# A second layer by block products behind a first layer: sums of x by a written plan, first block products right behind the first layer's last product, y matmuls 8, 10, 8, 10 between groups

## The chip, the cores and the metric

The program runs on one core of a Trainium2 chip. The metric is the time of one execution on the device in microseconds, as the median of runs; lower is better.

## The reference

Windowed attention with sink tokens gives x (1536 tokens, 512 wide). Two feed-forward layers follow, each 512 to 2048 to 512, the first with softplus, the second with hard swish:

```python
def _moe_ref(x, w_in, w_out):
    h = x @ w_in
    g = np.maximum(h, 0.0) + np.log1p(np.exp(-np.abs(h)))
    return (g @ w_out).astype(np.float32)

def _moe2_ref(x, w_in, w_out):
    h = x @ w_in
    relu6 = np.clip(h + 3.0, 0.0, 6.0)
    g = h * relu6 / 6.0
    return (g @ w_out).astype(np.float32)
```

The weights arrive as 64-bit floats.

## The kernel before

Every matmul operand is held as a high and a low half (hi + lo), and each product is made of three passes, hi hi, hi lo and lo hi. `xT` holds x transposed, four blocks of 128 features by 1536 tokens, both halves.

**First layer.** It goes over three token blocks of 512 (0 to 2) and in each over 16 chunks c of 128 hidden features: 48 steps, numbered 0 to 47; step 32 + c is chunk c of the last token block. `stage_a` of a step makes h (12 matmuls, `products`, L148) and the activation (`activate`, L170 to L180): ScalarE runs Abs, Exp, two copies and Ln, POOL makes u (L174), VectorE makes h (L177) and e (L178), ScalarE the high half of g (L179) and POOL the low half (L180). `stage_b` adds g times the second weight into four y banks (12 matmuls, L209), two steps later. Between Ln and L177 a call `filler` puts other work into the queues: in token blocks 1 and 2 that is `Blocks.early`. The four y banks of a token block are split into `xT` at its end (`evac`, L217 ScalarE, L218 VectorE); the second layer reads them there.

**Preparing the second layer.** `early` does three things. `some(n)` converts about n columns of the second layer's weights from 64-bit words on VectorE (L355, L359, L363; 32 weight pieces, and 48 groups of these three instructions, of 512 or 256 columns); L363 writes one tile f, which is written to DRAM (`kept`). `load` reads such pieces back. And in token block 2 the first block product's operands are made: `sums` (POOL, L401) and `left` (ScalarE L389 and POOL L390) from the weights, and `right(0)` from `xT`: eighteen VectorE sums (L451) in slots V and U, and eight splits of them (L389, L390). A split of V is read by ScalarE and POOL before the next sum may overwrite V. `right` is a generator; before, `early` takes two steps of it per chunk from chunk 3 on.

**Second layer.** It works on two halves of 768 tokens (s) with eight pairs of weight chunks each: 16 units (q = 0 to 15). A unit makes the 2 by 2 block product of the pair by seven products M1 to M7 in place of eight (L619, six matmuls of 128 by 384 each), in groups M1 M6, M2 M7, M5 M4, M3. Two PSUM banks take the products in turn, so M2 waits until M1's bank has been read, and so on. VectorE adds the products to the four quadrants of h (L601), and `act` turns a quadrant into g: ScalarE L529, VectorE L532 (its last reader of the bank), ScalarE L534, VectorE L536. Between the groups PE makes the 36 y matmuls of the unit before (`products` of `Blocks`, L571), so many that 11, 21, 31 and 36 of them are done behind the four groups. During units 1 to 7 `right(1)` makes the sums for the second token half, one generator step behind each group and two behind the second. In unit 8 the first half's six y banks are copied out (L589, L591).

At the seam, `Ffn.run(32, 48)` ends with the h of step 47 and the y of step 45; `Blocks.run` takes the 12 y matmuls of step 46 and then starts unit 0, between whose groups the 12 of step 47 stand.

From `with in_order` on, every engine's queue holds its instructions in the order in which the code issues them; the first layer's steps 4 to 31 are put in order by a scheduler.

## Time and profile before

| | us |
|---|---|
| median of 3 runs | 633.97 (632.43 to 636.32) |
| the profiled execution | 633.76 |
| its span, first to last instruction | 631.8 |
| PE busy | 602.9 (95%) |
| VectorE (DVE) busy | 432.4 (68%) |
| ScalarE (ACT) busy | 383.6 (61%) |
| POOL busy | 351.0 (56%) |
| mean granted PE clock | 0.993 |

PE's matmuls are pipelined: a row's duration counts from the first start to the last end, so what a block costs is read from one start to the next. The share of PE is an average; the stages differ, and the rows below are taken by stage. In a timeline row the bracket says how long the engine stood idle before it and what ended that.

### The profile page before, as it was taken

What the parts mean: (1) busy time and instruction counts of PE and PEld (TensorE: products, weight loads), DVE (VectorE), ACT (ScalarE), POOL (GpSimd) and SP (SyncE); (2) the same over time, 40 slices, a digit from 0 to 9 for tenths busy, and PEclk for the clock granted to TensorE, in tenths of its full rate; (3) what the DMA queues carried; (4) which work ended last, traced back from release to release, by engine and by line L of the source; (5) the groups of instructions that cost most, each with busy time, mean ns of one, the idle gap of its engine ahead of it and who ended that gap; (6) DMA issues with size and microseconds to landing.
All of it is one profiled execution on the core that took longest, in us unless ns stands there. A gap on an engine that the chain in (4) does not pass through costs nothing.

```text
span 631.8 us, 10989 instructions
## 1 busy us (share of the span) xinstructions
PE 602.9 (95%) x3863; PEld 509.3 (81%) x3863; DVE 432.4 (68%) x920; ACT 383.6 (61%) x843; POOL 351.0 (56%) x317
## 2 busy tenths in 40 slices
PE   8999999999999999989998869999999989999995
PEld 4888887887888888878876758988799878999984
DVE  6899999998788763377766457776755555555552
ACT  4999977887775566656666544554354444444432
POOL 1021248988544444535586755867786646666631
PEclk9999999999999999999999979999999999999999
DMA  7979869102656660043443210121212241211002
GB/s 218 274 235 279 268 222 365 41 0 93 203 188 198 202 200 1 1 133 101 129 156 115 84 35 33 66 68 67 67 66 67 84 150 67 68 67 34 1 1 106
DMA packets 54592, 75.12 MB, mean 119 GB/s; under 512 B 3904, under 2 KB 32576, under 8 KB 54528
## 3 DMA queue, kind: packets, MB, share of 16 engines
q1 hardware_dynamic: 53840, 74.07, 36.5%
q8 instruction: 32, 0.52, 0.3%
...
## 4 chain that ended last, share of the span: by engine, by line
PE 62%; DVE 13%; ACT 9%; POOL 6%; issue 4%; DMA 4%; SPq 0%; ACTq 0%; DVEq 0%; POOLq 0%
PE bank L619 15%; PE h_w L148 14%; PE y L571 14%; PE y_w L209 13%; PE bank L571 3%; POOL u_w L174 2%; ACT P L935 2%; DMA raw_w<-in_moe_w_in_dram 2%; DVE xs L931 1%; DVE e_w L178 1%; DVE slot_V L451 1%; PE o L973 1%; DVE e L532 1%; ACT e_w L171 1%; ACT u_w L173 1%
## 5 line engine op out<-in xcount | busy, mean ns | idle before, releaser
L209 PE MATMUL y_w<-g_w,w_w 128*128 128x512 f32 x576 | 142.9, 392 | 7.2 <-POOL g_w L180 4.8
L148 PE MATMUL h_w<-xT,w_w 128*128 128x512 f32 x576 | 140.9, 391 | 0.0
L209 PEld LDWEIGHTS y_w<-g_w,w_w 128*128 128x128 f32 x576 | 107.3, 188 | 32.8 <-POOL g_w L180 7.3
L148 PEld LDWEIGHTS h_w<-xT,w_w 128*128 128x128 f32 x576 | 107.6, 188 | 23.4 <-DVE e_w L178 0.9
L529 ACT ACTIVATE e<-bank 128x384 f32<-128x384 f32 x64 | 31.3, 492 | 108.6 <-DVE bank L601 107.7
L180 POOL TENSOR_TENSOR g_w<-e_w,g_w 128x512 fp32r<-128x512 f32 x48 | 62.8, 1308 | 51.2 <-ACT g_w L179 51.0
L174 POOL TENSOR_TENSOR u_w<-u_w,e_w 128x512 f32<-128x512 f32 x48 | 63.5, 1324 | 46.2 <-ACT u_w L173 45.1
L111 POOL TENSOR_TENSOR w_w<-t_w,w_w 128x512 fp32r<-128x512 f32 x32 | 41.4, 1294 | 64.5 <-ACT w_w L110 46.0
L571 PE MATMUL y<-slot_W,slot_G 128*128 128x512 f32 x279 | 72.8, 395 | 0.0
L179 ACT ACTIVATE g_w<-e_w 128x512 fp32r<-128x512 f32 x48 | 30.2, 630 | 62.7 <-DVE e_w L178 55.5
L571 PEld LDWEIGHTS y<-slot_W,slot_G 128*128 128x128 f32 x279 | 52.6, 190 | 10.1
L390 POOL TENSOR_TENSOR slot_B<-slot_S,slot_B 128x512 fp32r<-128x512 f32 x16 | 21.6, 1351 | 59.1 <-ACT slot_B L389 59.1
L177 DVE SCALAR_TENSOR_TENSOR h_w<-h_w,r_w 128x512 f32<-128x512 f32 x48 | 33.4, 695 | 29.3 <-ACT r_w L175 29.3
L571 PE MATMUL y<-slot_W,g 128*128 128x512 f32 x201 | 52.8, 392 | 0.0
L935 ACT ACTIVATE P<-xs,mx 128x208 f32<-128x208 f32 (+1 forms) x96 | 42.6, 447 | 10.6 <-DVE mx L931 10.4
L390 POOL TENSOR_TENSOR slot_W<-slot_O,slot_W 128x512 fp32r<-128x512 f32 x32 | 42.2, 1318 | 11.9 <-ACT slot_W L389 9.6
L571 PEld LDWEIGHTS y<-slot_W,g 128*128 128x128 f32 x201 | 37.5, 188 | 7.2
L532 DVE SCALAR_TENSOR_TENSOR e<-e,bank 128x384 f32<-128x384 f32 x64 | 34.9, 551 | 12.0 <-ACT e L529 11.2
L619 PE MATMUL bank<-xT,slot_C 128*128 128x384 f32 x192 | 39.2, 339 | 3.2 <-DVE e L532 3.2
L178 DVE TENSOR_TENSOR e_w<-h_w,u_w 128x512 f32<-128x512 f32 x48 | 33.1, 689 | 12.6 <-POOL u_w L174 12.0
L619 PE MATMUL bank<-xT,slot_A 128*128 128x384 f32 x192 | 39.3, 339 | 0.0
L619 PEld LDWEIGHTS bank<-xT,slot_C 128*128 128x128 f32 x192 | 34.0, 188 | 5.9 <-DVE e L532 4.9
(133 smaller groups left out, 1172.1 us busy)
## 6 DMA issues: line engine op xcount, KB each, us to landing
...
```

The lines of the kernel that those rows point to most:

```text
L111: nc.gpsimd.tensor_tensor(out=wt[:, 1, :], in0=t.bitcast(F32), in1=wt[:, 0, :].bitcast(F32), op=ALU.subtract)
L148: nc.tensor.matmul(h, wt[:, ws, kk * P : (kk + 1) * P], xT[:, xs, kk, t0 : t0 + 512], start=(n == 0), stop=(n == 11),)
L174: nc.gpsimd.tensor_tensor(out=u, in0=u, in1=e, op=ALU.subtract)
L177: nc.vector.scalar_tensor_tensor(out=h, in0=h, scalar=0.0, in1=r, op0=ALU.max, op1=ALU.add)
L178: nc.vector.tensor_tensor(out=e, in0=h, in1=u, op=ALU.subtract)
L180: nc.gpsimd.tensor_tensor(out=glo, in0=e, in1=ghi.bitcast(F32), op=ALU.subtract)
L209: yield nc.tensor.matmul(y, lhsT, rhs, start=(c == 0 and n == 0), stop=(c == 15 and n == 2))
L390: engine.tensor_tensor(out=lo.bitcast(F32R), in0=src, in1=hi, op=ALU.subtract)
L532: nc.vector.scalar_tensor_tensor(out=e, in0=e, scalar=6.0, in1=src, op0=ALU.min, op1=ALU.mult)
L571: nc.tensor.matmul(self.y[j], g[:, a, j % 3 * P : (j % 3 + 1) * P], wt[:, b * 512 : (b + 1) * 512], start=(p == 0 and io == 1 and n == 0), ...
L619: nc.tensor.matmul(h[m], a[x][kq], b[y][kq], start=(n == 0), stop=(n == 5))
L935: nc.scalar.activation(s["P", quad][:, hh, 0:w_], xs, AF.Exp, scale=-1.0, bias=s["mx"][:, h : h + 1], accum_out=s["sum"][:, h : h + 1],)
```

## The change

- **The plan.** `right` no longer runs as a generator in one fixed order. It returns a function that takes words: `a302` is two VectorE sums of the set 3 for k = 0, `s30` a split. The table `EARLY` gives the words per chunk 3 to 12 of the last token block, `LATE` those per unit and group. `left` and `sums` of the first block move to chunks 7 to 13, and the conversion is 2900 columns a step in token block 1 (2400 before) and 800 in token block 2 (1400).
- **The seam.** The first layer's loop ends at step 46. `Blocks.run` issues the h of step 47, then M1 and M6 of unit 0 with their two VectorE instructions and the sums of the next block, then step 47's activation. `rest(3)` now holds the 36 y matmuls of steps 45, 46 and 47, and they stand between the groups of unit 0 as those of a unit stand in every other.
- **The y matmuls** stand 8, 10, 8, 10 behind the four groups.
- **Places.** In unit 0 the small intermediate results lie in slots V and U; quadrants go first to slots G0 to G2, then to the two tiles shared with the first layer, and from unit 1 on also to G3 and G4. In unit 0 M1 is copied by VectorE, later by ScalarE as before. At the end of both halves outputs 2 to 5 lie in slots V and U.

```diff
-    def rest(self):
+    def rest(self, k):
...
-        for i in (n - 2, n - 1):
+        for i in range(n - k, n):
...
-        yield from t3(0)
-        last = t3(1)
-        yield next(last)
-        yield from part(f[0], b12[0])
...
+        def do(what):
+            for x in what.split():
+                if x[0] == "a":
+                    for _ in range(int(x[3])):
+                        next(adds[x[1]][int(x[2])], None)
+                else:
+                    src, to = part(x[1], int(x[2]))
+                    self.split(*to, src, self.nc.gpsimd)
+
+        return do
+
+    EARLY = {
+        3: "a303", 4: "a302 a311", 5: "s30 a313", 6: "s20 a311 a102", 7: "s31", 8: "s10 a112", 9: "s21 a402", 10: "s11",
...
+    LATE = {
+        (1, 0): "a301", (1, 1): "a301", (1, 2): "a301", (1, 3): "a302", (2, 0): "a311", (2, 1): "a311 s30",
...
-                self.some(2400)
+                self.some(2900)
...
-        self.some(1400)
+        self.some(800)
...
-        if c >= 3:
-            for _ in range(2):
-                next(self.t, None)
-        if c == 9:
+        if c in self.EARLY:
+            self.t(self.EARLY[c])
+        if c == 7:
             self.left(0, "A")
             self.load(1, 0)
-            self.load(0, 1)
-        elif c in (10, 11):
-            self.sums(0, c - 10)
-        elif 12 <= c <= 14:
-            self.left(0, "BCT"[c - 12])
+        elif c in (8, 9):
+            self.sums(0, c - 8)
+            if c == 9:
+                self.load(0, 1)
+        elif c in (10, 12, 13):
+            self.left(0, {10: "B", 12: "T", 13: "C"}[c])
...
-        if s == 0 or j < 2:
+        if j < 2:
             o = self.ffn.w.tmp.tile([P, 512], F32, tag="t", bufs=TB, name=f"o_{s}_{j}")
         else:
-            o = self.tmp.tile([P, 512], F32, tag="ru"[j // 2 - 1], bufs=2, name=f"o_{s}_{j}")
+            o = self.slots["VU"[j // 2 - 1]][:, j % 2 * 512 : j % 2 * 512 + 512]
...
+    YS = (8, 10, 8, 10)
...
-            upto = -(-total * done // 7)
-            while put < upto:
-                next(left, None)
-                put += 1
...
+    def run(self):
+        ffn = self.ffn
+        step = ffn.steps[-1]
+        ffn.products(step[0], *step[2:])
+        self.begin(ffn.rest(3))
+        self.group(0, 0)
+        ffn.activate(*step, lambda: ffn.filler(len(ffn.steps) - 1))
+        self.freed(15, 0)
+        self.more_g()
+        self.ys(0, 0)
+        for q in range(16):
+            for gi in range(4):
+                if (q, gi) != (0, 0):
+                    self.group(q, gi)
+                    self.ys(q, gi)
...
-            ffn.run(32, 48)
-            second.run(ffn.rest())
+            ffn.run(32, 47)
+            second.run()
```

How the queues differ is shown at three places. In names, the number behind `2_` in u, g, h and e is the chunk of the last token block.

POOL in the last token block, chunks 10 and 11 before: u and g of a step, and between them splits of the sums of x (xT, slot_E) and sums of the weights (slot_S).

```order
L174 TENSOR_TENSOR u_w1_2_10_4073<-u_w1_2_10_4073,e_w1_2_10_4071 128x512
L390 TENSOR_TENSOR xT_70<-slot_V_3564,xT_70 128x384
L390 TENSOR_TENSOR slot_E1_3726<-slot_U_3610,slot_E1_3726 128x384
L401 TENSOR_TENSOR slot_S_3933<-slot_I0_3669 128x256
L401 TENSOR_TENSOR slot_S_3933<-slot_S_3933,slot_I0_3669 128x256
L180 TENSOR_TENSOR g_w1_2_10_4070<-e_w1_2_10_4071,g_w1_2_10_4070 128x512
L174 TENSOR_TENSOR u_w1_2_11_4128<-u_w1_2_11_4128,e_w1_2_11_4126 128x512
L401 TENSOR_TENSOR slot_S_3933<-slot_I0_3669 128x256
L401 TENSOR_TENSOR slot_S_3933<-slot_I0_3669,slot_S_3933 128x256
L180 TENSOR_TENSOR g_w1_2_11_4125<-e_w1_2_11_4126,g_w1_2_11_4125 128x512
L174 TENSOR_TENSOR u_w1_2_12_4177<-u_w1_2_12_4177,e_w1_2_12_4175 128x512
L390 TENSOR_TENSOR slot_E2_3739<-slot_V_3564,slot_E2_3739 128x384
```
POOL now, chunks 8 and 9:

```order
L174 TENSOR_TENSOR u_w1_2_8_3992<-u_w1_2_8_3992,e_w1_2_8_3990 128x512
L390 TENSOR_TENSOR slot_E2_3769<-slot_V_3601,slot_E2_3769 128x384
L401 TENSOR_TENSOR slot_S_3962<-slot_I0_3699 128x256
L401 TENSOR_TENSOR slot_S_3962<-slot_S_3962,slot_I0_3699 128x256
L180 TENSOR_TENSOR g_w1_2_8_3989<-e_w1_2_8_3990,g_w1_2_8_3989 128x512
L174 TENSOR_TENSOR u_w1_2_9_4044<-u_w1_2_9_4044,e_w1_2_9_4042 128x512
L390 TENSOR_TENSOR slot_E1_3756<-slot_U_3646,slot_E1_3756 128x384
L401 TENSOR_TENSOR slot_S_3962<-slot_I0_3699 128x256
L401 TENSOR_TENSOR slot_S_3962<-slot_I0_3699,slot_S_3962 128x256
L180 TENSOR_TENSOR g_w1_2_9_4041<-e_w1_2_9_4042,g_w1_2_9_4041 128x512
```
The sums of the weights have moved from chunks 10 and 11 to 8 and 9, one split of x stands beside them in each, and no step holds two splits of x.

PE at the seam before: the last h of the first layer (chunk 15), then the y of chunks 13 and 14, then M1 and M6 (banks 0 and 1).

```order
L148 MATMUL h_w1_2_15_4321<-xT_70,w_w1_15_0_2564 128x512 x12
L209 MATMUL y_w1_2_0_3670<-g_w1_2_13_4230,w_w1_13_1_2517 128x512 x3
L209 MATMUL y_w1_2_1_3674<-g_w1_2_13_4230,w_w1_13_1_2517 128x512 x3
L209 MATMUL y_w1_2_2_3678<-g_w1_2_13_4230,w_w1_13_1_2517 128x512 x3
L209 MATMUL y_w1_2_3_3682<-g_w1_2_13_4230,w_w1_13_1_2517 128x512 x3
L209 MATMUL y_w1_2_0_3670<-g_w1_2_14_4284,w_w1_14_1_2572 128x512 x3
L209 MATMUL y_w1_2_1_3674<-g_w1_2_14_4284,w_w1_14_1_2572 128x512 x3
L209 MATMUL y_w1_2_2_3678<-g_w1_2_14_4284,w_w1_14_1_2572 128x512 x3
L209 MATMUL y_w1_2_3_3682<-g_w1_2_14_4284,w_w1_14_1_2572 128x512 x3
L619 MATMUL bank_0_4379<-xT_70,slot_A_3879 128x384 x6
L619 MATMUL bank_1_4380<-slot_E0_3686,slot_B_3946 128x384 x3
L619 MATMUL bank_1_4380<-slot_E1_3726,slot_B_3946 128x384 x3
```
PE at the seam now, from the same h on:

```order
L148 MATMUL h_w1_2_15_4325<-xT_70,w_w1_15_0_2564 128x512 x12
L623 MATMUL bank_0_4338<-xT_70,slot_A_3906 128x384 x6
L623 MATMUL bank_1_4339<-slot_E0_3716,slot_B_3975 128x384 x3
L623 MATMUL bank_1_4339<-slot_E1_3756,slot_B_3975 128x384 x3
L209 MATMUL y_w1_2_0_3700<-g_w1_2_13_4246,w_w1_13_1_2517 128x512 x3
L209 MATMUL y_w1_2_1_3704<-g_w1_2_13_4246,w_w1_13_1_2517 128x512 x3
L209 MATMUL y_w1_2_2_3708<-g_w1_2_13_4246,w_w1_13_1_2517 128x512 x2
L623 MATMUL bank_0_4338<-xT_70,slot_A_3906 128x384 x6
L623 MATMUL bank_1_4339<-xT_70,slot_C_4014 128x384 x6
L209 MATMUL y_w1_2_2_3708<-g_w1_2_13_4246,w_w1_13_1_2517 128x512
L209 MATMUL y_w1_2_3_3712<-g_w1_2_13_4246,w_w1_13_1_2517 128x512 x3
L209 MATMUL y_w1_2_0_3700<-g_w1_2_14_4293,w_w1_14_1_2572 128x512 x3
```
M1 and M6 have moved ahead of all y of chunks 13 and 14, and those y stand between the groups.

POOL at the seam before, from g of chunk 14 on: the sums of the next block's weights (slot_I1) stand behind all of the first layer.

```order
L180 TENSOR_TENSOR g_w1_2_14_4284<-e_w1_2_14_4285,g_w1_2_14_4284 128x512
L174 TENSOR_TENSOR u_w1_2_15_4337<-u_w1_2_15_4337,e_w1_2_15_4335 128x512
L390 TENSOR_TENSOR slot_E4_3793<-slot_V_3564,slot_E4_3793 128x384
L390 TENSOR_TENSOR slot_E5_3831<-slot_V_3564,slot_E5_3831 128x384
L180 TENSOR_TENSOR g_w1_2_15_4334<-e_w1_2_15_4335,g_w1_2_15_4334 128x512
L401 TENSOR_TENSOR slot_S_3933<-slot_I1_3844 128x256
L401 TENSOR_TENSOR slot_S_3933<-slot_S_3933,slot_I1_3844 128x256
L401 TENSOR_TENSOR slot_S_3933<-slot_I1_3844 128x256
L401 TENSOR_TENSOR slot_S_3933<-slot_I1_3844,slot_S_3933 128x256
```
POOL at the seam now, from the split of chunk 13 on:

```order
L390 TENSOR_TENSOR slot_C_4014<-slot_S_3962,slot_C_4014 128x512
L180 TENSOR_TENSOR g_w1_2_13_4246<-e_w1_2_13_4247,g_w1_2_13_4246 128x512
L174 TENSOR_TENSOR u_w1_2_14_4296<-u_w1_2_14_4296,e_w1_2_14_4294 128x512
L180 TENSOR_TENSOR g_w1_2_14_4293<-e_w1_2_14_4294,g_w1_2_14_4293 128x512
L401 TENSOR_TENSOR slot_S_3962<-slot_I1_3870 128x256
L401 TENSOR_TENSOR slot_S_3962<-slot_S_3962,slot_I1_3870 128x256
L401 TENSOR_TENSOR slot_S_3962<-slot_I1_3870 128x256
L401 TENSOR_TENSOR slot_S_3962<-slot_I1_3870,slot_S_3962 128x256
L174 TENSOR_TENSOR u_w1_2_15_4362<-u_w1_2_15_4362,e_w1_2_15_4360 128x512
L180 TENSOR_TENSOR g_w1_2_15_4359<-e_w1_2_15_4360,g_w1_2_15_4359 128x512
```
Splits of x are gone from chunk 15, and the four sums of the next block now stand ahead of u and g of chunk 15.

## Rows read from the trace of the kernel before

**Rows 1.** The page's chain that ended last, share of the span by engine.
```profile
PE 62%; DVE 13%; ACT 9%; POOL 6%; issue 4%; DMA 4%; SPq 0%; ACTq 0%; DVEq 0%; POOLq 0%
```
**Rows 2.** Windows: stretch, length, busy us of each engine (instructions), PE clock, DMA.
```profile
271.69:342.76 71.07, 69.03 (x300) 56.27 (x301) 51.43 (x86) 46.55 (x82) 41.36 (x35) 1.00 0.42 134
342.76:366.76 24.00, 20.01 (x91) 15.99 (x90) 13.33 (x22) 12.87 (x24) 15.72 (x16) 1.00 0.22 77
366.76:389.01 22.25, 18.08 (x80) 15.87 (x79) 14.19 (x24) 10.57 (x22) 11.22 (x11) 0.85 0.14 47
389.01:522.39 133.38, 127.83 (x626) 112.81 (x625) 83.47 (x138) 63.92 (x133) 94.22 (x90) 1.00 0.22 76
522.39:538.08 15.69, 15.69 (x79) 14.14 (x79) 8.50 (x15) 7.36 (x16) 10.05 (x11) 1.00 0.20 68
538.08:624.70 86.62, 86.61 (x426) 77.09 (x425) 45.02 (x79) 38.33 (x78) 47.21 (x46) 1.00 0.11 36
```
**Rows 3.** Timeline of PE: start, us, line, operation, count, [idle before].
```profile
320.81 2.88 PE L209 MATMUL y_w<-g_w,w_w 128*128 128x512 f32 x12
...
323.53 2.88 PE L148 MATMUL h_w<-xT,w_w 128*128 128x512 f32 x12
...
327.49 2.80 PE L209 MATMUL y_w<-g_w,w_w 128*128 128x512 f32 x11 [0.85 <-POOL g_w L180]
...
372.15 2.29 PE L619 MATMUL bank<-slot_E,slot_B 128*128 128x384 f32 x6 [4.17 <-DVE e L532]
```
**Rows 4.** Timeline of POOL, chunks 10 and 11 of the last token block.
```profile
320.90 1.30 POOL L174 TENSOR_TENSOR u_w<-u_w,e_w 128x512 f32<-128x512 f32 x1 [1.25 <-ACT u_w L173]
...
322.15 1.02 POOL L390 TENSOR_TENSOR xT<-slot_V,xT 128x384 fp32r<-128x384 f32 x1
...
325.85 1.59 POOL L180 TENSOR_TENSOR g_w<-e_w,g_w 128x512 fp32r<-128x512 f32 x1
```
**Rows 5.** Timeline of VectorE, last token block.
```profile
280.03 0.42 DVE L363 SCALAR_TENSOR_TENSOR f<-raw,m 128x256 int32<-128x256 int32 x1 [1.21 <-DMA kept<-f]
...
280.95 1.53 DVE L451 TENSOR_TENSOR slot_V<-slot_V,xT 128x384 f32<-128x384 f32 x1
...
286.51 0.56 DVE L451 TENSOR_TENSOR slot_U<-slot_V,xT 128x384 f32<-128x384 f32 x1
...
334.99 1.63 DVE L451 TENSOR_TENSOR slot_V<-xT,slot_U 128x384 f32<-128x384 f32 x1 [3.80 <-POOL slot_E L390]
```
**Rows 6.** Groups by line, POOL: out<-in, count, busy us, mean ns.
```profile
L401 POOL TENSOR_TENSOR slot_S<-slot_I 128x256 f32<-128x256 f32 x32 | 24.2, 756 | 0.0
```
**Rows 7.** Timeline, ScalarE and VectorE, one step without other work.
```profile
264.97 0.58 ACT L170 ACTIVATE e_w<-h_w 128x512 f32<-128x512 f32 x1
...
269.01 0.69 DVE L178 TENSOR_TENSOR e_w<-h_w,u_w 128x512 f32<-128x512 f32 x1 [0.21 <-POOL u_w L174]
...
269.79 0.63 ACT L179 ACTIVATE g_w<-e_w 128x512 fp32r<-128x512 f32 x1 [1.73 <-PE h_w L148]
```
**Rows 8.** Timeline of unit 11, VectorE and PE.
```profile
543.82 0.57 DVE L601 TENSOR_TENSOR bank<-bank,c 128x384 f32<-128x384 f32 x1 [2.97 <-PE bank L619]
...
545.33 0.55 DVE L532 SCALAR_TENSOR_TENSOR e<-e,bank 128x384 f32<-128x384 f32 x1
...
549.07 1.55 PE L571 MATMUL y<-slot_W,slot_G 128*128 128x512 f32 x6
...
549.88 1.13 DVE L532 SCALAR_TENSOR_TENSOR e<-e,bank 128x384 f32<-128x384 f32 x2
```
**Rows 9.** Timeline where units 8 and 9 meet, VectorE and PE; outputs are copied.
```profile
505.09 0.69 DVE L591 COPY o<-y 128x512 f32<-128x512 f32 x1 [2.19 <-PE bank L619]
...
507.48 1.33 PE L619 MATMUL bank<-slot_F,slot_B 128*128 128x384 f32 x6 [2.51 <-DVE e L532]
```
**Rows 10.** VectorE's group in 150 to 262; then the window 233 to 262.
```profile
L355 DVE TENSOR_SCALAR m<-raw 128x256 int32<-128x256 int32 (+1 forms) x31 | 16.1, 520 | 3.9 <-DMA raw<-in_moe_w_out_dram 1.6 <-DMA raw<-in_moe_w_in_dram 1.6
...
233.00:262.00 29.00, 29.00 (x130) 24.01 (x129) 7.82 (x12) 19.33 (x34) 14.89 (x12) 1.00 0.09 28
```

More of the change, by code (lines that the diff above doesn't have):

```diff
@@ L543, in begin, with room, more_g @@
         self.m, self.y = three[0:2], three[2:3]
[L544 to L548 removed]
+        self.gs = self.room(0, 3)
         self.which = 0
+        self.u = {}
         self.g = {}
         self.before = tail
+    def room(self, a, b):
+        return [
+            self.slots[f"G{i}"].bitcast(F32R).rearrange("p (a f) -> p a f", a=2)[:, :, 0:384] for i in range(a, b)
+        ]
+    def more_g(self):
+        self.gs += [
+            self.tmp.tile([P, 2, 512], F32R, tag="g", bufs=2, name=f"g2_{i}")[:, :, 0:384] for i in range(2)
+        ]
     def banks(self):
@@ L592, in evac, with group @@
         nc.sync.dma_start(self.out[t0 : t0 + P, :], o)
-    def unit(self, s, p):
+    GROUPS = (("M1", "M6"), ("M2", "M7"), ("M5", "M4"), ("M3",))
+    YS = (8, 10, 8, 10)
+    def group(self, q, gi):
         nc, tmp = self.nc, self.tmp
-        last = s == 1 and p == 7
-        q = 8 * s + p
-        nm = f"{s}_{p}"
+        s, p = divmod(q, 8)
+        last = q == 15
+        h = {}
+        for m in self.GROUPS[gi]:
+            h[m], a, b = self.m[self.which][:, 0:384], self.lhs(m), self.rhs(s, m)
+            self.which = 1 - self.which
+            n = 0
+            for kq in range(2):
+                for x, y in PASSES:
+                    nc.tensor.matmul(h[m], a[x][kq], b[y][kq], start=(n == 0), stop=(n == 5))
+                    n += 1
@@ L664, in unit, with small @@
-        for _ in left:
-            pass
-        self.before = self.products(s, p, dict(self.g))
-    def run(self, tail):
-        for _ in range(12):
-            next(tail)
-        self.begin(tail)
-        for s in range(2):
-            for p in range(8):
-                self.unit(s, p)
+        def small(n):
+            if q == 0:
+                t, x = "VU"[n in (3, 4)], n in (2, 4)
+                self.u[n] = self.slots[t][:, x * 512 : x * 512 + 384]
+            else:
+                self.u[n] = tmp.tile([P, 512], F32, tag="ru"[n in (3, 4)], bufs=2, name=f"u{n}_{q}")[:, 0:384]
+            return self.u[n]
@@ new lines, in group @@
+        u = self.u
+        if gi == 0:
+            if q == 0:
+                nc.vector.tensor_copy(small(1), h["M1"])
+            else:
+                nc.scalar.activation(small(1), h["M1"], AF.Copy)
+            add(small(2), h["M6"], u[1])
+            if q:
+                self.outs(q - 1, 0)
+            if not last:
+                self.sums(q + 1, 0)
+                self.sums(q + 1, 1)
+            if 0 < q < 14:
+                self.load(q + 2, 0)
+                self.load(q + 2, 1)
+        elif gi == 1:
+            add(h["M2"], h["M2"], u[1])
+            add(small(3), h["M7"], u[2])
+            self.act((h["M2"], (0, 0), q))
+            if not last:
+                self.left(q + 1, "A")
+        elif gi == 2:
+            add(small(4), h["M5"], u[2])
+            add(h["M5"], h["M5"], u[3])
+            add(h["M4"], h["M4"], u[3])
+            self.act((h["M5"], (1, 1), q), (h["M4"], (1, 0), q))
+            if not last:
+                self.left(q + 1, "B")
+            self.outs(q, 1)
+            if not last:
+                self.left(q + 1, "T")
+        else:
+            add(h["M3"], h["M3"], u[4])
+            self.act((h["M3"], (0, 1), q))
+            if not last:
+                self.left(q + 1, "C")
@@ new lines, in group, with ys @@
+        if q == 1 and gi == 0:
+            self.t = self.right(1)
+        if (q, gi) in self.LATE:
+            self.t(self.LATE[q, gi])
+    def ys(self, q, gi):
+        for _ in range(self.YS[gi]):
+            next(self.before, None)
+        if gi < 3:
+            return
+        for _ in self.before:
+            pass
+        if q == 0:
+            self.gs += self.room(3, 5)
+        self.before = self.products(*divmod(q, 8), dict(self.g))
+    def run(self):
[13 more added lines that the diff above has]
+                    self.ys(q, gi)
```

99 lines of the change are left out of this document (16 added, 83 removed), and 3 rows, old and new, of the table LATE.

## The prediction

> **What bounds the kernel now.** I read the shares of the chain of waits first: TensorE carries 62% of it, and VectorE, ScalarE and POOL follow [rows 1]. So TensorE (PE) is the bound, and what a change can win is the time in which it waits. The windows by stage say where that is [rows 2]. A second-layer unit with no wait takes 15.69 us (522.39 to 538.08), with PE busy for all of it; the five units behind it and the last 36 y matmuls take 86.62, which leaves 86.62 - 5 x 15.69 = 8.17 for the 36, or 0.227 a matmul. The seven products of a unit then cost 15.69 - 8.17 = 7.52, or 1.07 each. A first-layer group of 12 matmuls starts 2.72 after the one before it [rows 3]. With these four numbers each window has a length without waits:
> - 271.69 to 342.76: 25 groups of 12, 68.0 of 71.07. Lost 3.1.
> - 342.76 to 366.76 (the last h product, the y of steps 45 to 47, unit 0): 2.72 + 36 x 0.227 + 7.52 = 18.4 of 24.00. Lost 5.6.
> - 366.76 to 389.01, unit 1: 15.69 of 22.25. Lost 6.6.
> - 389.01 to 522.39, units 2 to 9: 125.5 of 133.38. Lost 7.9.
> - From 522.39 on: nothing.
> That is 23.2 us, in the steps ahead of the seam of the two layers, at the seam and in the units behind it.
>
> What is waited for stands in PE's timeline [rows 3]. At 327.49 it is POOL's low half of g. The longest wait, 4.17 at 372.15, is for VectorE in unit 1, and behind it six matmuls take 2.29 where an undisturbed block needs 1.07, and the window's granted clock reads 0.85 [rows 2, 3]: the two levels are 1.2 and 2.4 GHz, and PE ran at the lower one for some us after it had stood still. That extra, about 2, belongs to the wait and goes with it. POOL has no gap from 320.90 to 327.44: u, two splits, two sums and the low half of g in one step [rows 4]. VectorE waits 3.80 at 334.99 for a POOL split that still reads slot V [rows 5].
>
> **Part 1, the sums of x by a plan.** Before, two of the eight splits of x stand in steps 38 and 39, and the other six with all sums of the weights and three of their four splits are bunched in steps 42 to 47; the plan puts one split of x into each of the steps 37 to 44 and the sums into 40 and 41. The order of POOL shows it. The loads of a step: POOL needs 1.30 for u and as much for g when nothing disturbs it [rows 4]; the heaviest planned steps (40 and 41) add one split of 1.02 [rows 4] and two sums of 0.75 [rows 6], so 2 x 1.30 + 1.02 + 1.50 = 5.1 of the 5.44 that PE takes. Before, step 42 had 2 x 1.30 + 2 x 1.02 + 1.50 = 6.1, and that is the step whose g came late at 327.49. The chain ScalarE, POOL, VectorE, ScalarE closes once a step: Abs at 264.97, the next pass to the high half at 269.79, 0.63 long [rows 7], so 5.4 against 5.44: a step that is late stays late. A late g is noticed by PE only when it is not there 4 x 2.72 = 10.9 after its h; Abs to high half 4.82, its 0.63 and POOL's 1.3 make 6.8, about 1 more when splits stand ahead of it. So a step may be about 3 late before PE waits. Before, two things made it late ahead of the bunch: f waiting for the write of the f before it to DRAM (1.21 at 280.03 [rows 5]) and the bunch itself. The plan gives VectorE fewer conversion columns here (800 for 1400), which leaves more than a step between the write and the next f, so I take that wait as gone. VectorE has 5.4 a step less h and e at 0.69 each [rows 7], so 4.0; conversion at 0.42 for 256 columns [rows 5], 1.3 to 1.4 with the rounding up, and three sums at 0.56 are 3.1. The split that VectorE waited for at 334.99 is now issued a step ahead of the sum that overwrites its source. I expect the 3.1 of the first window to go but for the 0.16 with which PE restarted at 271.69, and charge 0.3: 2.6 won.
>
> One row speaks against this. A sum of x in SBUF takes 0.56 when POOL is idle and took 1.53 at 280.95, beside a POOL instruction [rows 5]; where the two engines take turns, steps 40 and 41 need 5.1 + 2 x 0.56 = 6.2 of 5.44, each 0.8 late, 1.6 together. That stays under the 3, so PE does not see it there; it is handed on to the seam, and I charge it there in part. The Trainium skill has this as a rule (SBUF — State Buffer, "Who interferes with whom"): a VectorE instruction with two inputs in SBUF and a POOL instruction that reads SBUF exclude each other for the whole instruction. By that rule every one of these sums would take its turn, the full 1.6 would reach the seam, and the time would be about 0.9 above my sum; by the row at 286.51 alone it would be 0.6 below.
>
> **Part 2, the seam.** The last h is followed at once by M1 and M6; all three last first-layer steps then give 36 y matmuls between the groups of unit 0, where before 24 of them stood ahead of M1 and PE waited for each g in turn. Counted from the start of the last h: h to 2.72, M1 and M6 to 4.9, 8 y to 6.7, M2 and M7 to 8.8, 10 y to 11.1, then M5. M6's bank is free when e of step 46 is done. That step's h ended at -2.72; I allow 0.4 of lateness, and from Abs to the end of e are 4.7 [rows 7], so it is done at 2.4, and PE asks at 3.8: margin 1.4. M5's bank is free when unit 0's first quadrant is through VectorE, and that stands behind e of step 47, which waits for POOL: low half of g46 to 4.45, four sums of the next block at 0.75 to 7.5, u47 at 1.30 to 8.8, e47 at 0.69 to 9.5, then add, ScalarE, VectorE, 1.6 without the wait for M7 in the row at 543.82 to 545.88 [rows 8]: 11.2. PE asks at 11.1. So 0.1 without lateness; with the 1.6 from part 1 it is 1.7, of which M6 would wait 0.2. I take 0.9, the middle, since the row of a sum beside POOL shows both. Quadrants go first to slots of their own (G0 to G2), so the wait of g for y of step 47, which held unit 0's ScalarE, is gone, and with it the 4.17 of unit 1 and its slow clock. In unit 1 the four evacuations of the first layer's last y stand on VectorE ahead of u2. From M3's end to M7 PE has 18 y, M1, M6 and M2, 7.3 us; M3's own chain of 1.6, its two halves at 0.6 each, four evacuations at 0.69 (as e, the same size) and u2 at 0.57 make 6.1: in time, no charge.
>
> **Part 3, y 8, 10, 8, 10 in place of 11, 10, 10, 5.** Behind M3 there is now 10 x 0.227 + 1.07 = 3.3 before M6 wants its bank, before 2.2; that answers the smaller waits for M3's last reader in units 2 to 5. The place that gets tighter is behind M4, 8 for 10. There y starts at 549.07 and M5's last reader is done at 549.88 + half of 1.13 = 550.44, 1.4 later [rows 8]; 8 y are 1.8. Margin 0.4, so steady units keep 15.69. A sum of x ahead of it in units 1 to 7 can use that up; I charge 0.4 over all. That the sums are moved to other gaps costs nothing more: they hide under 15.69 of PE with VectorE at 8.5 [rows 2].
>
> **Part 4, evacuation at the turn of the halves.** VectorE's copy at 505.09 waited 2.19, and it writes one of two buffers from which an earlier output is still being written to DRAM, and PE got M6's bank at 507.48 [rows 9]. Now the six outputs have six places, so the copies wait for y alone. Of the 7.9 lost in units 2 to 9 this is 2.5. I charge 0.2 for the copies that still stand ahead of M3's add.
>
> **Part 5, 2900 for 2400 conversion columns in the middle block.** 15 steps x 500 = 7500 columns move there. The code counts 100 more than its columns for an instruction, so the 48 groups (16 of 3 x 612, 32 of 3 x 356) are 1324 each on average, and 5.7 of them move. Before, 31 groups begin in 150 to 262 and none after 233, where VectorE's 12 instructions are the h and e of six steps, 7.82 busy of 29 with PE at 29.00 [rows 10]. So a group takes 83 / 31 = 2.7; six more end near 249, before the block does. Cost nothing; the cover is 13 us of a VectorE that is mostly idle.
>
> **Sum.** The profiled execution took 633.76 (span 631.8 and 1.96 around it), against a median of 633.97. 633.76 - (3.1 + 5.6 + 6.6 + 7.9) + 0.16 + charges 0.3 + 0.9 + 0.4 + 0.2 = 612.5. Its own range is 609.5 (no charge at all, and some of the wait at 271.69 gone too) to 617.
>
> **The rivals.** (a) The seam inherits the old lateness: POOL's plan is no lighter in truth and a step stays 3 late. Then the 2.6 of part 1 stay lost, M6 waits 1.3 and M5 1.6: 612.5 + 2.6 + 2.0 = 617.1; with a stand long enough to lower the clock again 619. For it: the 1.53 at 280.95; against: 5.1 of 5.44.
> (b) Eight y behind M4 are too few: if splits or sums push VectorE by 0.7 in every unit, 0.3 over the margin, 15 units cost 4.5: 617. Against: the 0.4 of rows 8.
> (c) The change doesn't do all it says: some waits in units 1 to 9 have other causes than I read, and half of their 14.5 stays: 619.7.
> (d) Slower: the conversions of the middle block overrun it. f has one tile, and each group waits for the write of the one before; the one at 280.03 took 1.21, and I allow 1.5. If all 37 groups waited 1.5 beyond their present 2.7 they would take 155 from 150 on, end at 305 instead of by 262, and hold up h and e for 43 us: 612.5 + 43 = 655. It decides from 0.9 a group: 13 / 37 = 0.35 uses up the cover, 21 / 37 = 0.57 the gain. Against: the idle window of rows 10.
>
> **How the numbers follow.** Forecast 0.68, (a) 0.11, (b) 0.08, (c) 0.10, (d) 0.03. A measurement of this kernel tells about 1%, 6.3 us, from no change. The forecast, (a), (b) and nearly all of (c) are beyond it: faster 0.95; same 0.02; slower 0.03. The range of 8 in 10 takes in the forecast's own and reaches to (a), (b) and (c): 609.0 to 620.
>
> **What would show it.** Right: no PE wait on POOL's g between 300 and 345; after the last h M1 with no wait, M5 with one of 0 to 2; unit 1 near 15.7 with the clock at 1.00; no wait near 500 for a copy of outputs; steady units at 15.69. Wrong: waits for e at M6 of unit 0, a wait at M3 in every unit, conversions running beside steps 32 to 36, or a lowered clock behind the seam.

## The result

The changed kernel takes 616.33 us (median of 4 runs, 614.22 to 617.62) against 633.47 (632.43 to 636.32): a ratio of 0.9719, 95% interval 0.9677 to 0.9762. The prediction was 612.5, 0.966 of 633.97. The direction and the range hold; the number is about 4 us too low.

| | before | after |
|---|---|---|
| the profiled execution, us | 633.76 | 617.62 |
| its span | 631.8 | 615.8 |
| PE busy | 602.9 (95%) | 600.6 (98%) |
| VectorE busy | 432.4 (68%) | 434.7 (71%) |
| ScalarE busy | 383.6 (61%) | 383.8 (62%) |
| POOL busy | 351.0 (56%) | 353.9 (57%) |
| mean granted PE clock | 0.993 | 0.993 |

The work is the same; it is packed more tightly. The chain that ended last, to compare with [rows 1]:

```profile
PE 79%; DVE 8%; ACT 5%; DMA 3%; issue 2%; POOL 2%; SPq 0%; POOLq 0%; ACTq 0%; DVEq 0%
```

PE's share of the chain rose from 62% to 79%, and POOL's fell to 2%. PE's timeline of after shows where the prediction held and where it did not (start, us, line, operation, count, [idle before]; M products are L623 now, y L586):

```profile
266.61 2.88 PE L148 MATMUL h_w<-xT,w_w 128*128 128x512 f32 x12
273.26 5.49 PE L209 MATMUL y_w<-g_w,w_w 128*128 128x512 f32 x12 [3.77 <-DVE xT L218]
278.55 3.14 PE L148 MATMUL h_w<-xT,w_w 128*128 128x512 f32 x12
281.53 2.88 PE L209 MATMUL y_w<-g_w,w_w 128*128 128x512 f32 x12
...
344.09 2.88 PE L148 MATMUL h_w<-xT,w_w 128*128 128x512 f32 x12
346.81 1.23 PE L623 MATMUL bank<-xT,slot_A 128*128 128x384 f32 x6
347.88 1.20 PE L623 MATMUL bank<-slot_E,slot_B 128*128 128x384 f32 x6
...
355.65 1.31 PE L623 MATMUL bank<-slot_E,slot_B 128*128 128x384 f32 x6 [0.31 <-DVE e L540]
...
363.07 1.23 PE L623 MATMUL bank<-xT,slot_A 128*128 128x384 f32 x6
...
378.90 1.23 PE L623 MATMUL bank<-xT,slot_A 128*128 128x384 f32 x6
```

From 281.53 to 344.09 are 62.56, exactly 23 groups of 2.72: the waits of [rows 3] are gone. M1 follows the last h at once; M5 waits a little; unit 1 takes 15.83 instead of 22.25. But at the turn from token block 1 to 2 (y of step 32 at 273.26) PE stands 3.9 where it stood 2.1 before, and the 12 matmuls behind it take 5.29 from start to start. The same place before:

```profile
266.91 2.88 PE L148 MATMUL h_w<-xT,w_w 128*128 128x512 f32 x12
271.69 3.05 PE L209 MATMUL y_w<-g_w,w_w 128*128 128x512 f32 x12 [1.89 <-DVE xT L218]
```

The windows of after give the clock there (stretch, length, busy us of PE, its weight loads, VectorE, ScalarE, POOL, then clock and DMA):

```profile
269.00:273.20 4.20, 0.49 (x3) 0.07 (x1) 2.08 (x4) 2.49 (x6) 2.39 (x2) 0.89 0.32 116
273.20:278.50 5.30, 5.24 (x12) 4.13 (x13) 4.30 (x10) 3.65 (x7) 1.43 (x2) 0.50 0.00 0
```

The clock is 0.50 behind the stand: the 1.2 GHz level. Together the turn costs 6.8 us, before 2.2.

**Where PE loses time, in all runs.** The table is worked as in the prediction, from starts of PE's rows in each profiled execution: a first-layer group without waits is 2.72, a unit 15.69, last h to unit 1's M1 18.41. "Turn" is the stand ahead of step 32's y, plus what the next two groups take beyond 5.44. The runs are explained below.

| run | turn | to the last h | last h to unit 1 | unit 1 | units 2 to 9 | median us |
|---|---|---|---|---|---|---|
| before | 2.06 + 0.16 | 2.91 | 5.59 | 6.56 | 7.70 | 633.47 |
| after | 3.93 + 2.83 | 0 | 0.57 | 0.14 | 1.27 | 616.33 |
| before_2900 | 3.30 + 1.78 | 0.43 | 5.32 | 5.95 | 7.72 | 633.98 |
| cols_back | 1.86 + 0.14 | 0.82 | 2.89 | 0.15 | 1.29 | 616.59 |
| hi_first | 2.30 + 0.14 | 0 | 0.60 | 0.14 | 1.26 | 613.61 |
| hi_2400 | 0.52 + 0.12 | 0.86 | 2.89 | 0.15 | 1.23 | 614.99 |
| plan_old | 3.94 + 1.75 | 0.43 | 4.69 | 0.14 | 1.24 | 619.78 |
| ys_old | 4.07 + 1.77 | 0 | 0 | 1.89 | 1.25 | 617.70 |
| evac_old | 4.00 + 2.43 | 0 | 0.57 | 0.12 | 2.46 | 618.28 |
| seam_old | 3.32 + 2.91 | 0 | 1.92 | 4.27 | 0.46 | 621.51 |
| best_a | 2.85 + 0.13 | 0 | 0.57 | 0.02 | 1.97 | 615.44 |
| best_b | 0.53 + 0.15 | 0 | 0.84 | 0.02 | 1.96 | 612.58 |
| best_c | 1.04 + 0.13 | 0 | 0.29 | 0.16 | 0.38 | 610.07 |

Each ratio below is against executions of the kernel before taken beside that run; their medians were 633.3 to 635.3. After, plan_old, ys_old, evac_old and seam_old are alike up to the turn and yet lose 5.7 to 6.8 there; so a microsecond between two medians decides little, and the columns are compared one by one. One slow run of seam_old, 3363.44 us, is left out of its ratio.

### The profile page after: what moved, and what is told of

Read it like the earlier page. It is cut to its first block, busy times and chain, and to the rows that moved or that the text cites. A ratio compares the mean times of both kernels' runs of the same rounds, so it can differ in the third digit from the quotient of the medians.

```text
span 615.8 us, 10950 instructions
## 1 busy us (share of the span) xinstructions
PE 600.6 (98%) x3863; PEld 510.2 (83%) x3863; DVE 434.7 (71%) x921; ACT 383.8 (62%) x842; POOL 353.9 (57%) x317
## 4 chain that ended last, share of the span: by engine, by line
PE 79%; DVE 8%; ACT 5%; DMA 3%; issue 2%; POOL 2%; SPq 0%; POOLq 0%; ACTq 0%; DVEq 0%
PE bank L623 19%; PE y_w L209 19%; PE h_w L148 17%; PE y L586 17%; PE bank L586 4%; ACT P L964 2%; DVE xs L960 2%; POOL u_w L174 1%; DMA raw_w<-in_moe_w_out_dram 1%; PE spare L1039 1%; DMA v<-in_v_dram 1%; DMA raw_w<-in_moe_w_in_dram 1%; DVE t_w L103 1%; DVE x L1017 1%; DVE e_w L178 1%
## 5 line engine op out<-in xcount | busy, mean ns | idle before, releaser
L209 PEld LDWEIGHTS y_w<-g_w,w_w 128*128 128x128 f32 x576 | 109.3, 191 | 28.4 <-DVE xT L218 4.2
L586 PE MATMUL y<-slot_W,slot_G 128*128 128x512 f32 x336 | 85.7, 392 | 0.0
L586 PEld LDWEIGHTS y<-slot_W,slot_G 128*128 128x128 f32 x336 | 62.9, 188 | 12.8
L179 ACT ACTIVATE g_w<-e_w 128x512 fp32r<-128x512 f32 x48 | 30.3, 630 | 62.9 <-DVE e_w L178 53.8
L627 DVE TENSOR_TENSOR bank<-bank,u 128x384 f32<-128x384 f32 x60 | 33.2, 561 | 24.4 <-PE bank L623 24.0
L627 DVE TENSOR_TENSOR u<-bank,u 128x384 f32<-128x384 f32 x45 | 25.0, 555 | 32.9 <-PE bank L623 18.1
L623 PE MATMUL bank<-xT,slot_C 128*128 128x384 f32 x192 | 39.3, 339 | 0.2
L623 PE MATMUL bank<-xT,slot_A 128*128 128x384 f32 x192 | 39.3, 340 | 0.0
L586 PE MATMUL y<-slot_W,g 128*128 128x512 f32 x144 | 37.3, 392 | 0.0
```

What stands on the lines that cost most here:

```text
L209: yield nc.tensor.matmul(y, lhsT, rhs, start=(c == 0 and n == 0), stop=(c == 15 and n == 2))
L586: nc.tensor.matmul(self.y[j], g[:, a, j % 3 * P : (j % 3 + 1) * P], wt[:, b * 512 : (b + 1) * 512], start=(p == 0 and io == 1 and n == 0), ...
L623: nc.tensor.matmul(h[m], a[x][kq], b[y][kq], start=(n == 0), stop=(n == 5))
L627: nc.vector.tensor_tensor(out=out, in0=in0, in1=in1, op=ALU.add)
```

## Why the turn came late

ScalarE's copies of y to `xT` (L217) stand in its queue behind the copy to g's high half (L179) of step 33, and that waits for VectorE's e. So the chain ScalarE, POOL, VectorE sets when PE may go on. ScalarE's rows of L179 in after, one for each step, and at the end those of step 33 and of the copies behind it:

```profile
234.12 0.63 ACT L179 ACTIVATE g_w<-e_w 128x512 fp32r<-128x512 f32 x1 [1.86 <-DVE e_w L178]
...
240.80 0.63 ACT L179 ACTIVATE g_w<-e_w 128x512 fp32r<-128x512 f32 x1 [3.25 <-DVE e_w L178]
...
246.13 0.63 ACT L179 ACTIVATE g_w<-e_w 128x512 fp32r<-128x512 f32 x1 [1.99 <-DVE e_w L178]
...
251.18 0.63 ACT L179 ACTIVATE g_w<-e_w 128x512 fp32r<-128x512 f32 x1 [1.71 <-DVE e_w L178]
...
271.37 0.63 ACT L179 ACTIVATE g_w<-e_w 128x512 fp32r<-128x512 f32 x1 [1.71 <-DVE e_w L178]
271.90 2.04 ACT L217 ACTIVATE xT<-y_w 128x512 fp32r<-128x512 f32 x4
```

The step to 240.80 takes 6.7. VectorE's rows say why: h and e stand among conversions, two of which wait, for a weight piece from DRAM and for the write of f.

```profile
237.33 0.69 DVE L355 TENSOR_SCALAR m<-raw 128x512 int32<-128x512 int32 x1 [0.58 <-DMA raw<-in_moe_w_out_dram]
237.94 0.69 DVE L177 SCALAR_TENSOR_TENSOR h_w<-h_w,r_w 128x512 f32<-128x512 f32 x1
238.53 0.69 DVE L359 SCALAR_TENSOR_TENSOR m<-raw,m 128x512 int32<-128x512 int32 x1
239.47 0.69 DVE L363 SCALAR_TENSOR_TENSOR f<-raw,m 128x512 int32<-128x512 int32 x1 [0.26 <-DMA kept<-f]
240.08 0.68 DVE L178 TENSOR_TENSOR e_w<-h_w,u_w 128x512 f32<-128x512 f32 x1
```

Without conversions a step of the chain takes 5.05 (246.13 to 251.18) against PE's 5.44, so it gains 0.39 a step. The same rows of before, where the conversions have ended:

```profile
234.44 0.63 ACT L179 ACTIVATE g_w<-e_w 128x512 fp32r<-128x512 f32 x1 [1.71 <-DVE e_w L178]
...
239.49 0.63 ACT L179 ACTIVATE g_w<-e_w 128x512 fp32r<-128x512 f32 x1 [1.64 <-DVE e_w L178]
...
249.60 0.63 ACT L179 ACTIVATE g_w<-e_w 128x512 fp32r<-128x512 f32 x1 [0.87 <-DVE e_w L178]
```

At 249.60 against 251.18, with PE 0.3 earlier in after (266.61 against 266.91), the chain is 1.9 later. It keeps this distance up to step 33 (269.79 in [rows 7] against 271.37), and 3.93 - 2.06 is that 1.9. The quiet stretch of [rows 10] was not spare: in it the chain caught up. Most of the 1.9 comes from one step: 234.44 to 239.49 is 5.05 before, 234.12 to 240.80 is 6.68 after, 1.6 more. All eight kernels with 2900 columns have such a step (6.4 to 7.0); the other kernels with 2400 take 5.05 there too, and those with 2600 5.3 to 5.5. So the lateness is taken on mostly in one step, in which conversions and their waits for DRAM stand ahead of e; which of the two weighs more, no run separates.

## The experiments

**The columns put back (cols_back), and the columns alone (before_2900).**

```diff
-                self.some(2900)
+                self.some(2400)
...
-        self.some(800)
+        self.some(1400)
```

> The changed kernel with 2400 and 1400 conversion columns a step, as before the change; its plan, seam, y counts and evacuation places stay. Theory A (the extra columns set VectorE's h and e back in the middle block, so the chain ScalarE, POOL, VectorE comes late to the turn of the token blocks and the first layer's copies stand behind it): PE's wait for xT at the turn falls from 3.8 to about 2, the 12 matmuls behind it take 2.7 to 3 instead of 5.3, and the time falls by 4 to 4.6, to about 612. Rival B (the stand at the turn comes from the plan or from the order that holds from step 32 on, not from the number of columns): wait still 3.8, time 616. Rival C (the columns cost in the last block what they save at the turn): the wait at the turn falls to 2, but waits for g come back between the turn and the seam, 2 to 4 in all; time 614 to 616.

> The kernel before with only the conversion columns changed, 2900 in the middle block and 800 in the last. Theory A: the wait at the turn grows from 1.9 to 3.8 and the clock falls behind it, 4.5 more; of the 3.1 lost between the turn and the last h some comes back because fewer columns are left there, 0 to 2; time 634 to 638. Rival B: wait at the turn stays at 1.9, time 631 to 633.5.

cols_back took 616.59, ratio 0.9711 (0.9683 to 0.9740); before_2900 633.98, ratio 0.9986 (0.9967 to 1.0005). PE in cols_back:

```profile
271.33 3.02 PE L209 MATMUL y_w<-g_w,w_w 128*128 128x512 f32 x12 [1.70 <-DVE xT L218]
...
345.49 1.31 PE L623 MATMUL bank<-slot_E,slot_B 128*128 128x384 f32 x6 [1.25 <-DVE e_w L178]
...
354.18 1.31 PE L623 MATMUL bank<-slot_E,slot_B 128*128 128x384 f32 x6 [1.11 <-DVE e L540]
```

The turn follows the columns in both kernels, so rival B is out. But what the turn gives back, 4.8, is mostly lost again: 0.8 ahead of the last h and 2.3 at the seam, where M6 now waits 1.25 for e of step 46 and M5 1.11. That the 1400 columns of the last block cost this, and not PE's earlier return, is seen in hi_first below: its stand is nearly as short, with 800 columns, and it loses nothing ahead of the last h and 0.6 at the seam. Theory A was right on the place and rival C on the price; the 1.6 that remain are within the spread of after's own runs (3.4), and 616.59 is not told apart from 616.33. before_2900 shows the same from the other side, 2.9 more at the turn and 2.5 less between it and the last h.

**ScalarE's copies ahead of the waiting one (hi_first), and both edits (hi_2400).** Only step 33 differs; the y of step 31 stay where they were on PE.

```diff
+        def filler():
+            for j in range(4):
+                self.evac(key, kind, blk, self.out, j, "hi")
+            self.filler(s)
+
+        self.activate(*self.steps[s], filler)
+        for j in range(4):
+            self.evac(key, kind, blk, self.out, j, "lo")
```

> The changed kernel with 2900 and 800, but at the turn of the middle and last token block ScalarE's four copies of y to the high half of xT stand behind step 33's logarithm and ahead of its copy to the high half of g; VectorE's four low halves stay behind e of that step. Theory A: ScalarE has the copies in the 1.7 in which it waits for e, so xT's first low half ends about 1.3 earlier; PE's wait falls from 3.8 to about 2.5 and the clock may stay up; time 612 to 615. Rival B: the wait is for y or for the conversions and not for ScalarE's place in the queue; wait 3.8, time 616.

> Both edits: 2400 and 1400 columns, and the copies ahead of g's high half at the turn. Theory A: the wait at the turn falls to 0.1 to 0.8 and the clock stays at 1.00; time 610 to 611.5. Rival C: waits for g come back between the turn and the seam and the time is 613 or more.

hi_first took 613.61, ratio 0.9672 (0.9642 to 0.9702); hi_2400 614.99, 0.9687 (0.9659 to 0.9715). In hi_first ScalarE fills its gap (the copy is L218 there), and PE stands 2.3 with no loss of clock behind it:

```profile
269.40 2.04 ACT L218 ACTIVATE xT<-y_w 128x512 fp32r<-128x512 f32 x4
271.31 0.65 ACT L179 ACTIVATE g_w<-e_w 128x512 fp32r<-128x512 f32 x1
```
```profile
271.77 3.02 PE L209 MATMUL y_w<-g_w,w_w 128*128 128x512 f32 x12 [2.14 <-DVE xT L220]
274.63 2.88 PE L148 MATMUL h_w<-xT,w_w 128*128 128x512 f32 x12
```

So the queue's order was part of the stand. The interval of hi_first overlaps that of the changed kernel; that it is faster is shown by its turn, 2.44 for 6.76, with the other columns alike. hi_2400 has almost no stand left (0.52) and still is no faster than hi_first, because it loses 0.9 ahead of the last h and 2.9 at the seam: rival C again.

**The plan undone (plan_old)**: the old sequence of the 26 words and the old chunks of `left`, `sums` and `load`, with 2900 and 800 columns.

```diff
-        3: "a303", 4: "a302 a311", 5: "s30 a313", 6: "s20 a311 a102", 7: "s31", 8: "s10 a112", 9: "s21 a402", 10: "s11",
-        11: "s40 a412", 12: "s41",
+        3: "a302", 4: "a302", 5: "a301 a311", 6: "s30 a311", 7: "s20 a311", 8: "a312", 9: "a102", 10: "s31 s21",
+        11: "a112", 12: "s10 a401", 13: "a401 s11", 14: "a412 s40 s41",
```

> The changed kernel with the old order of the sums and splits of x (two in a step from step 35 on, and the last splits in step 46 instead of 47), of the splits and sums of the weights and of their loads in the last block; columns stay at 2900 and 800. The prediction's part 1 (the plan removes the waits): 2.6 come back between the turn and the last h, and 2.0 at the seam as in its rival (a); 619 to 621. Theory C (what removed those waits was the columns, since before_2900 with the old plan lost only some 0.4 from 280 to the last h): 0 to 0.6 there, 1 to 2.5 at the seam because the bunch in steps 42 to 46 makes the chain late; 617 to 619.

619.78, ratio 0.9762 (0.9732 to 0.9792).

```profile
349.55 1.32 PE L622 MATMUL bank<-slot_E,slot_B 128*128 128x384 f32 x6 [1.99 <-DVE e_w L178]
...
359.28 1.33 PE L622 MATMUL bank<-slot_E,slot_B 128*128 128x384 f32 x6 [2.14 <-DVE e L539]
```

With 2900 and 800 columns the plan is worth 0.43 ahead of the last h. With 2400 and 1400 it is worth 2.1 there, from 2.91 before to 0.82 in cols_back; so either edit alone takes most of the 2.91 away. At the seam the plan is worth 4.1, about twice what either theory gave: the bunched splits leave the chain late, and M6 and M5 pay. The time lies in the range of part 1, but the loss in another place. The interval overlaps that of the changed kernel; the seam's rows tell the two apart.

**The old y counts (ys_old).**

```diff
-    YS = (8, 10, 8, 10)
+    YS = (11, 10, 10, 5)
```

> The changed kernel with 11, 10, 10, 5 y matmuls between the groups of a second-layer unit. The prediction's part 3 (the five behind M3 are too few while sums of x run): waits for M3's last reader come back in units 1 to 6, 3.5 to 5 in all, and the 0.3 that units 2 to 5 now lose behind M4 goes; 618.5 to 620. Rival (the waits came from where the sums stood, behind M4 and in every group, and the new places cure them alone): units 1 to 6 near 15.7, time 615 to 616.5. The steady units stay at 15.7 in both.

617.70, ratio 0.9721 (0.9683 to 0.9759), not told apart from after. Units 2 to 9 lose 1.25 in all, as in after, but not in the same units: units 2 to 6 lose 0.7 for 1.2, and unit 9, where outputs are copied, 0.5 where after loses nothing. Unit 1 loses 1.75 more, with five y behind M3, and the seam 0.57 less. Units 1 to 6 together lose 2.6: less than the 3.5 to 5 of part 3, more than the rival's. Before, units 2 to 6 lost 4.9; the counts did not cure that. The rival's cause, the new places of the sums, is likely, but no run puts these places back.

**The old output places (evac_old).**

```diff
-        if j < 2:
+        if s == 0 or j < 2:
...
-            o = self.slots["VU"[j // 2 - 1]][:, j % 2 * 512 : j % 2 * 512 + 512]
+            o = self.tmp.tile([P, 512], F32, tag="ru"[j // 2 - 1], bufs=2, name=f"o_{s}_{j}")
```

> The changed kernel with the old places of the outputs at the turn of the halves: the six of the first half in two buffers, the last four of the second half in r and u. The prediction's part 4: VectorE's copies wait again for the writes to DRAM, 2.2 each, and unit 9 takes 18.2 to 18.5 instead of 15.7; 618.5 to 619. Rival (with other y counts the copies no longer stand ahead of a bank that PE wants): unit 9 at 15.7 to 16.3, time 616 to 617.

618.28, ratio 0.9745 (0.9712 to 0.9777); unit 9 takes 16.92 instead of 15.71. VectorE's copy, ScalarE's copy and PE:

```profile
494.29 0.69 DVE L606 COPY o<-y 128x512 f32<-128x512 f32 x1 [2.18 <-DMA out_dram<-o]
```
```profile
493.51 0.60 ACT L604 ACTIVATE o<-y 128x512 f32<-128x512 f32 x1 [2.17 <-DMA out_dram<-o]
```
```profile
494.55 1.34 PE L623 MATMUL bank<-xT,slot_A 128*128 128x384 f32 x6 [0.94 <-ACT u L642]
```

VectorE's wait is as long as the one of [rows 9], 2.18 for 2.19, but PE no longer hangs on it. It waits for ScalarE's copy of M1 (u), which stands behind a copy of an output that waited 2.17 for a write to DRAM, and it loses 1.2 by it: an outcome between the two expectations. With the old counts the new places are worth more: unit 9 took 18.49 before and takes 16.20 in ys_old.

**The old seam (seam_old)**: y of steps 45 and 46 ahead of M1, and 4, 3, 4, 1 of step 47's y between the groups of unit 0.

```diff
-        ffn.products(step[0], *step[2:])
-        self.begin(ffn.rest(3))
+        tail = self.ffn.rest(2)
+        for _ in range(12):
+            next(tail)
+        self.begin(tail)
...
-            ffn.run(32, 47)
+            ffn.run(32, 48)
```

> The changed kernel with the old seam: the y of steps 45 and 46 stand ahead of M1, and only the 12 of step 47 between the groups of unit 0 (4, 3, 4, 1); slots for the quadrants, evacuation places and the rest stay as changed. The prediction's part 2: from the last h to unit 1's M1 PE takes 23 to 24 instead of 18.4 to 19, because each y waits for its g; unit 1 stays near 15.8 since its quadrants have slots of their own; 620 to 622. Rival (the old chain was only late because of the old plan, and waits for g are gone): 19 to 20 from the last h to unit 1, time 616 to 618.

621.51, ratio 0.9785 (0.9747 to 0.9823). PE, then VectorE, then ScalarE:

```profile
362.79 1.31 PE L623 MATMUL bank<-xT,slot_C 128*128 128x384 f32 x6 [1.12 <-DVE e L540]
364.17 1.22 PE L623 MATMUL bank<-xT,slot_A 128*128 128x384 f32 x6
368.01 2.29 PE L623 MATMUL bank<-slot_E,slot_B 128*128 128x384 f32 x6 [2.63 <-DVE e L540]
```
```profile
365.62 0.69 DVE L218 TENSOR_TENSOR xT<-y_w,xT 128x512 fp32r<-128x512 f32 x1 [1.27 <-ACT xT L217]
366.23 0.56 DVE L627 TENSOR_TENSOR bank<-bank,slot_U 128x384 f32<-128x384 f32 x1
```
```profile
365.01 0.58 ACT L217 ACTIVATE xT<-y_w 128x512 fp32r<-128x512 f32 x1
```

The total is what part 2 expected, but in other places: 1.35 at the seam and 4.1 in unit 1. This is the 372.15 of [rows 3] again, with six matmuls taking 2.29. With slots of their own for the quadrants the wait is still there: one y stands behind M3, and M6 wants M3's bank before VectorE has read it.

The rows show what keeps VectorE from it. M3 is done by 364.1, but its sum (L627) starts at 366.23, and VectorE stands idle for 1.27 of the time between. Ahead of the sum in its queue stands the low half of one of the first layer's last four y banks (365.62), which waits for ScalarE's high half (365.01), which is queued behind three splits of weights. Before it was the same:

```profile
369.76 0.69 DVE L218 TENSOR_TENSOR xT<-y_w,xT 128x512 fp32r<-128x512 f32 x1 [1.21 <-ACT xT L217]
```

The code puts the copies of a y bank into the queues right behind the issue of its last matmul. With one y of step 47 left behind M3, three of the four banks' copies are issued ahead of M3's sum; with five left (ys_old) two are; with ten (after) none, and there all four run behind M3's quadrant:

```profile
364.36 2.48 DVE L218 TENSOR_TENSOR xT<-y_w,xT 128x512 fp32r<-128x512 f32 x4 [0.45 <-ACT xT L217]
```

Unit 1 loses 4.27, 1.89 and 0.14 in the three. No run moves the copies alone, so what they cost is not measured apart from the cover that the y give PE.

**Towards a better version.** best_a adds two edits to hi_first: the sum behind M2 in units 1 to 6 goes behind M3, and the four sums of weights in unit 0 go behind M2's quadrant. best_b adds columns in between (2600; 2000 in steps 32 to 34, then 800). best_c moves the sums of x only from unit 3 on, and puts all 12 y of step 45 behind M6.

```diff
-        for _ in range(self.YS[gi]):
+        for _ in range((12, 6, 8, 10)[gi] if q == 0 else self.YS[gi]):
```

> The copies ahead of g's high half at the turn (as in hi_first, 2900 and 800 columns), and two more edits. The sum of x that stood behind M2's quadrant in units 1 to 6 stands behind M3's: in units 2 to 5 such a sum took 1.65 beside POOL's splits, ahead of u4, where it takes 0.55 when POOL is idle. And the four sums of the next block's weights in unit 0 stand behind M2's quadrant and no longer ahead of the u of step 47 on POOL. If VectorE and POOL hold each other up as that 1.65 says, units 1 to 5 fall from 15.83 to 16.0 to 15.7, 1.3 in all; if the time behind M4 was short for another reason they stay near 16.0 or the wait moves to M7. Unit 0 falls from 16.29 to 15.7 to 15.9. Together 611.7 to 612.2 against 613.6; with neither effect 613.6.

> As best_a, with the columns in between: 2600 a step in the middle block, 2000 in steps 32 to 34, 800 from step 35 on. Theory A: the wait at the turn falls from 2.1 to 1 to 1.5; if the steps from 35 on give the chain time to catch up, unit 0 stays near 15.8 and the time is 610.8 to 611.5. Theory C (lateness taken on in the last block is kept to the seam): M6 and M5 wait 0.5 to 2 there and the time is 612 or more.

> As best_b, with two edits. The sums of x keep the changed kernel's places in units 1 and 2 and stand behind M3's quadrant only from unit 3 on, so that no unit has three of them ahead of u2: best_a's wait of 0.63 for u at M7 in units 2 and 3 goes, unit 2 falls from 16.6 to 16.0, units 3 to 5 to 15.7, 1.4 in all. And in unit 0 all 12 y of step 45 stand behind M6, 6 behind M7: if M5's 0.31 is ScalarE's copy to g of step 47, which uses the place of step 45's g and so waits for its last y, with the first quadrant queued behind it, unit 0 falls from 16.5 by 0.5 to 0.8; if M5 waits for the u or e of step 47, it stays. Together 611.2 or a little less against 612.6 for best_b; without the second effect 611.6.

best_a took 615.44, ratio 0.9716 (0.9686 to 0.9746): a miss. Units 1, 4 and 5 fall to 15.7, but units 2 and 3 rise to 16.6, because three sums beside POOL's splits now stand ahead of u2. PE and VectorE there:

```profile
381.44 1.33 PE L644 MATMUL bank<-xT,slot_C 128*128 128x384 f32 x6 [0.63 <-DVE u L648]
```
```profile
377.82 1.53 DVE L472 TENSOR_TENSOR slot_U<-slot_V,xT 128x384 f32<-128x384 f32 x1
...
380.84 0.54 DVE L648 TENSOR_TENSOR u<-bank,u 128x384 f32<-128x384 f32 x1
```

And M5's 0.31 stays, although e of step 47 now starts 4.3 behind M1's start and no longer 5.9. ScalarE in after, and in best_c, tells who holds it:

```profile
354.00 0.63 ACT L179 ACTIVATE g_w<-e_w 128x512 fp32r<-128x512 f32 x1 [3.81 <-PE y_w L209]
354.54 0.47 ACT L537 ACTIVATE e<-bank 128x384 f32<-128x384 f32 x1
```
```profile
348.13 0.63 ACT L179 ACTIVATE g_w<-e_w 128x512 fp32r<-128x512 f32 x1 [1.74 <-DVE e_w L178]
348.67 0.47 ACT L558 ACTIVATE e<-bank 128x384 f32<-128x384 f32 x1
```

Step 47's g takes the place of step 45's and waits for its last y; the first quadrant is queued behind it. With those y done first, M5 no longer waits. best_b took 612.58, ratio 0.9674 (0.9656 to 0.9691): its stand at the turn falls to 0.53, lower than expected, but the seam takes 0.84 and units 2 and 3 stay at 16.6, which is theory C's time. best_c took 610.07 (5 runs, 609.96 to 610.58), ratio 0.9625 (0.9600 to 0.9649), about 1 less than expected, and this lies below the interval of the changed kernel: the fastest version here, with 2.0 us lost in the table against 8.7.

## Right and wrong, point by point

- **Part 5, "Cost nothing; the cover is 13 us of a VectorE that is mostly idle"** is the step that failed. The conversions ended by 246, as estimated (249), and the block was not overrun; but one step took 6.7, and the idle stretch was the chain's time to catch up, 0.39 a step. The prediction had worked out a period of 5.4 from [rows 7], so that a late step stays late; that is a step of the part in issue order (266.03 to 271.37 in after is 5.34). In the middle block, in the order of the scheduler, it is 5.05 in both traces. The turn cost 4.5 more, of that 1.9 for the longer stand and 2.7 for the clock behind it. 612.5 + 4.5 is 617.0, beside 617.62 for the profiled run. The wait at 271.69 was taken as a constant, and who ended it was never followed up: ScalarE's queue, and ahead of that VectorE's e.
- **Part 1**: its window lost nothing (charged 0.3). Both reasons given, the plan and the fewer columns, hold there, and either alone does most of it: the plan 2.1 with the old columns and 0.43 with the new ones, the columns 2.5 with the old plan (before_2900, where the longer stand at the turn may help too). With the new columns the plan's worth, 4.1, lies at the seam, which is rival (a)'s place with twice its size.
- **Part 2**: charged 0.9, measured 0.57, with M5's wait in the range of 0.1 to 1.7. The chain behind it was not the four sums on POOL and u47 (best_a took them away and nothing changed), but g47 behind step 45's y. The 4.17 of unit 1 was put down to g's slots. seam_old has the slots and still stands 2.63 and loses 4.27; so most of it belongs to the few y behind M3 and to the first layer's copies on VectorE ahead of M3's sum. The prediction saw these copies ahead of u2 in the changed kernel, where they cost nothing, and not in the old one.
- **Part 3**: charged 0.4, measured 1.3 in units 1 to 5. The place was right, a sum of x ahead of M5's and M4's chain; the size was not. The gain in units 2 to 6 did not come from the counts (ys_old); that it came from the places of the sums is not shown by a run of its own.
- **Part 4**: charged 0.2, nothing measured; the places are worth 1.2 with the new counts (evac_old), and 2.3 with the old ones, unit 9 of before against ys_old; 2.5 was expected.
- **The rivals**: (b) came in small, 0.3 in four units. Of (c)'s 14.5 only 1.4 stayed, not half. (d) had the right cause and the wrong mechanism: the conversions never overran the block.
- **Luck**: the four charges add up to 1.8, and their places lost 1.9, though three of the four are off by more than half. And the range reached to 620 for rivals (a) to (c); the 4 that were missing come from a place that none of them names.
